# The order of three matmul terms in an MLP with split operands

## The chip, the core and the metric

The kernel runs on one core of a Trainium2 chip. The metric is the device time of the whole program in microseconds, from runs of the same program. One more execution was recorded by the hardware profiler, and everything that is said of instructions, waits and cadences is read from that record.

## What is computed

Sigmoid attention over 8 batches, 12 heads, 448 positions and a head size of 64, and then an MLP without biases on the 3584 rows that come out of it (768 to 2048 to 768, with a sigmoid-approximated GELU between):

```python
scores = scale * np.matmul(q, k.transpose(0, 1, 3, 2)) - np.log(S)
attn = 1.0 / (1.0 + np.exp(-scores))
x = np.matmul(attn, v)            # then (B, S, H * D) -> (3584, 768)
h = x @ w_in                      # 768 x 2048
g = h * (1.0 / (1.0 + np.exp(-1.702 * h)))
out = g @ w_out                   # 2048 x 768
```

## The kernel before, in words

The program has two halves. Up to about 253 us TensorE does the attention, while the other engines decode the weights. After that comes the MLP, which the change touches. The MLP does not multiply the matrices as they stand: it uses a fast bilinear scheme with 26 products per pair of blocks, so VectorE adds and subtracts blocks of the weights (`ws`, `kw`, `wf`), of the activations (`x`, `xs`, `kx` for the first matrix, `gs`, `kg`, `gl` for the second) and of the results (`h`, `o`). The table `SEQUENCE` lists 104 such products in the order in which TensorE takes them: two groups of tokens, two matrices, 26 products.

Each product needs two operands in more than one piece of precision. `split_piece` (lines 805 to 816) makes from a block of weights a tile `w` with a rounded part (index 0, "high", written by ScalarE at line 810 or VectorE at line 811) and what the rounding left (index 1, "low", a subtraction on VectorE at line 813, which can begin only when the high part is there). `pair_of` (lines 1021 to 1062) makes from a block of activations a tile `xp` (first matrix) or `gp` (second matrix) in the same way: high at lines 1040, 1041 or 1046, low on VectorE at line 1052 or 1054. Everything that is named `xp`, `gp` and `w` in the profile is such a tile.

`matmuls` (lines 841 to 848) then multiplies. For each 128x128 block of weights and each stretch of 448 columns of activations it issues three matmuls that add into the same place: the table `TERMS` (line 44) gives, for each of the three, which part of the weights (`a`) and which part of the activations (`d`) is read. Low times low is left out. A product is 36 matmuls in one go: 12 blocks by 3 terms. All 104 products together are 3744 matmuls with 128x128 weights, 1872 for each matrix.

The list scheduler `Plan.run` decides the order on each engine before anything runs, with its own estimates. A product's tasks on TensorE depend on the tasks that write the low parts, which come last, so the order is planned as if a product could begin only when both low parts are there. What each instruction waits for at run time is not set by the planner: it is put in afterwards, tile by tile and part by part, from what the instruction really reads. The matmul that reads a part first carries the wait for it, and everything behind it on TensorE's queue waits with it.

Other waits at the start of a product come from the accumulators: the two PSUM tiles `h0` and `h1` (named `p` in the profile) are used in turn, and a product can begin only when ScalarE or VectorE has read the one before it out (line 1228 a copy, 1262 an addition). Some products add to a value that ScalarE first copies in (lines 1186, 1188).

```python
            for j, (a, d) in enumerate(TERMS):
                nc.tensor.matmul(
                    ps, lhsT=ws(c // 6)[:, a, c % 6 * P : (c % 6 + 1) * P], rhs=x[:, d, k], start=start and i == 0 and j == 0,
                    stop=stop and i == len(todo) - 1 and j == 2, skip_group_check=True,
                )
```

Of the kernel before, what the change touches and what calls it, by code (L numbers as in the profile page):

```python
# [40 lines left out]
ISSUE, LANDING, PER_KB, MM = 0.43, (2.2, 2.5), 0.0027, 0.203  # L41
PIECE_RATE = dict(load=0.0032, save=0.0027)

TERMS = ((0, 1), (1, 0), (0, 0))

W_SUMS = ([(8, 0, 1, -1), (9, 5, 7, 1), (10, 3, 7, 1), (11, 0, 4, -1), (12, 0, 2, -1), (13, 6, 9, -1), (14, 4, 8, -1), (15, 6, 10, -1), (16, 2, 8, -1), (17, 10, 11, -1), (18, 4, 13, 1), (19, 3, 16, -1), (20, 9, 12, -1), (21, 6, 11, -1), (22, 6, 7, -1), (23, 5, 14, -1), (24, 1, 9, -1), (25, 2, 15, 1)], [(9, 1), (19, 1), (14, -1), (16, -1), (3, 1), (17, -1), (8, 1), (2, 1), (22, -1), (6, -1), (11, -1), (3, 1), (25, 1), (4, 1), (1, -1), (12, -1), (24, -1), (13, -1), (5, -1), (20, 1), (21, -1), (2, -1), (10, -1), (23, 1), (15, 1), (18, -1)])
X_SUMS = ([(8, 3, 7, 1), (9, 2, 6, 1), (10, 0, 3, 1), (11, 4, 6, -1), (12, 5, 9, 1), (13, 0, 8, 1), (14, 5, 6, 1), (15, 1, 3, -1), (16, 1, 8, -1), (17, 4, 9, -1), (18, 4, 13, 1), (19, 1, 12, 1), (20, 0, 17, 1), (21, 2, 10, -1), (22, 10, 14, 1), (23, 7, 11, 1), (24, 5, 16, 1), (25, 11, 15, 1)], [(9, -1), (14, 1), (13, 1), (22, 1), (5, -1), (16, 1), (10, -1), (21, 1), (11, 1), (20, 1), (8, 1), (23, 1), (15, 1), (0, 1), (18, 1), (19, 1), (5, 1), (17, 1), (4, -1), (12, -1), (1, -1), (1, -1), (24, -1), (7, -1), (25, 1), (2, 1)])
# [341 lines left out]
def sigmoid_attention_mlp(ctx: ExitStack, tc: tile.TileContext, qk, v, w, out):  # L389
# [451 lines left out]
    def matmuls(ps, ws, x, todo, start, stop):  # L841

        for i, (c, k) in enumerate(todo):
            for j, (a, d) in enumerate(TERMS):
                nc.tensor.matmul(  # L845
# [467 lines left out]
```

## Time and profile before

| | |
|---|---|
| median of the runs | 1045.49 us (2 runs, 1045.29 to 1045.7) |
| the profiled execution's own time | 1043.49 us |
| its span | 1041.7 us |
| granted clock of TensorE | 1.0 |
| matmuls and weight loads | 5588 and 5588 |
| busy share of PE, PEld, DVE, ACT | 98%, 80%, 90%, 56% |

PE is TensorE's matmuls and PEld its weight loads, which are recorded apart and overlap the matmuls. DVE is VectorE, ACT is ScalarE, SP issues the DMAs. A matmul's recorded duration is longer than the distance to the next one, because they are pipelined: the distance from start to start (here called the cadence) says what one costs. Idle time counts only where the chain of work that ends last runs through it.

### The profile page before, as it was taken

What the parts mean: (1) busy time and instruction counts of PE and PEld (TensorE: products, weight loads), DVE (VectorE), ACT (ScalarE), POOL (GpSimd) and SP (SyncE); (2) the same over time, 40 slices, a digit from 0 to 9 for tenths busy, and PEclk for the clock granted to TensorE, in tenths of its full rate; (3) what the DMA queues carried; (4) which work ended last, traced back from release to release, by engine and by line L of the source; (5) the groups of instructions that cost most, each with busy time, mean ns of one, the idle gap of its engine ahead of it and who ended that gap; (6) DMA issues with size and microseconds to landing.
All of it is one profiled execution on the core that took longest, in us unless ns stands there. A gap on an engine that the chain in (4) does not pass through costs nothing. (4 is left out here: it accounts for less than half of the span.)

```text
span 1041.7 us, 13721 instructions
## 1 busy us (share of the span) xinstructions
PE 1024.7 (98%) x5588; PEld 832.3 (80%) x5588; DVE 933.7 (90%) x654; ACT 588.4 (56%) x473; POOL 0.2 (0%) x4
## 2 busy tenths in 40 slices
PE   9999999999999999999999999999999999999998
PEld 5545454555898988888898898989999999999987
DVE  6998898897889988898899698999999999999896
ACT  6888887784454556545535445645563336454553
POOL 0000000000000000000000000000000000000000
PEclk9999999999999999999999999999999999999999
DMA  9999998879879878897997885966668389756755
GB/s 349 365 340 379 352 349 306 313 269 320 329 286 379 355 264 307 327 371 290 353 335 265 308 315 184 367 256 224 272 218 343 131 314 378 289 192 235 264 211 222
DMA packets 62799, 310.63 MB, mean 298 GB/s; under 512 B 6544, under 2 KB 14864, under 8 KB 58896
## 3 DMA queue, kind: packets, MB, share of 16 engines
q1 hardware_dynamic: 62736, 309.75, 79.4%
q8 instruction: 44, 0.72, 0.3%
q14 instruction: 19, 0.16, 0.0%
HBM read 200.38 MB, written 109.35 MB: 297 GB/s over the span
## 5 line engine op out<-in xcount | busy, mean ns | idle before, releaser
L845 PE MATMUL p<-xp,w 128*128 128x448 f32 x1872 | 386.1, 367 | 11.4 <-DVE xp L1052 7.5
L845 PEld LDWEIGHTS p<-xp,w 128*128 128x128 f32 x1872 | 349.8, 188 | 47.9 <-issue 10.2
L845 PE MATMUL p<-gp,w 128*128 128x448 f32 x1872 | 387.5, 368 | 0.3 <-DVE gp L1052 0.2
L845 PEld LDWEIGHTS p<-gp,w 128*128 128x128 f32 x1872 | 351.0, 188 | 36.3 <-issue 0.8
L635 ACT ACTIVATE a<-sc,bias 128x896 f32<-128x896 f32 x168 | 156.2, 1015 | 42.8 <-PE sc L665 26.2
L680 PE MATMUL av<-a,vraw 128*64 128x448 f32 x576 | 113.5, 543 | 0.0
L1228 ACT COPY h<-p 128x1792 f32<-128x1792 f32 x30 | 49.7, 1657 | 106.7 <-PE p L845 65.0
L1228 ACT COPY o<-p 128x1344 f32<-128x1344 f32 x37 | 47.1, 1283 | 101.8 <-PE p L845 95.5
L1262 DVE TENSOR_TENSOR h<-h,p 128x1792 f32<-128x1792 f32 x40 | 79.8, 2016 | 21.3 <-ACT h L1228 18.7
L649 PEld LDWEIGHTS sc<-qk 64*128 64x128 f32 x846 | 75.6, 184 | 27.7 <-PE sc L665 16.2
L649 PE MATMUL sc<-qk 64*128 64x448 f32 x846 | 94.7, 373 | 0.7 <-DVE x L710 0.7
L680 PEld LDWEIGHTS av<-a,vraw 128*64 128x64 f32 x576 | 39.2, 137 | 63.3 <-issue 46.8
L1262 DVE TENSOR_TENSOR o<-o,p 128x1344 f32<-128x1344 f32 x34 | 52.2, 1549 | 7.5 <-ACT o L1228 5.1
L1089 ACT ACTIVATE h<-h 128x1792 f32<-128x1792 f32 x28 | 47.5, 1702 | 14.5 <-DVE h L1262 14.5
L519 DVE TENSOR_TENSOR qk<-qkraw,qk 128x896 fp32r<-128x896 f32 x47 | 50.5, 1085 | 0.6
L1052 DVE TENSOR_TENSOR xp<-x,xp 128x1344 fp32r<-128x1344 f32 x26 | 40.4, 1552 | 8.1 <-ACT xp L1040 7.9
L710 DVE COPY x<-av 128x896 f32<-128x896 f32 x23 | 25.1, 1089 | 18.6 <-PE av L693 18.6
L1052 DVE TENSOR_TENSOR gp<-gs,gp 128x1792 fp32r<-128x1792 f32 x19 | 38.4, 2022 | 2.6 <-ACT gp L1040 2.2
L1052 DVE TENSOR_TENSOR gp<-kg,gp 128x1792 fp32r<-128x1792 f32 x18 | 36.3, 2019 | 1.7 <-ACT gp L1040 1.5
L813 DVE TENSOR_TENSOR w<-ws,w 128x1536 fp32r<-128x1536 f32 x19 | 33.3, 1752 | 1.3 <-ACT w L810 1.1
L514 DVE CAST qk<-qkraw 128x896 fp32r<-128x896 f32 x37 | 22.8, 622 | 12.4 <-DMA qkraw<-qk 6.1
L813 DVE TENSOR_TENSOR w<-kw,w 128x1536 fp32r<-128x1536 f32 x18 | 31.5, 1752 | 2.6 <-ACT w L810 2.6
(109 smaller groups left out, 931.8 us busy)
## 6 DMA issues: line engine op xcount, KB each, us to landing
w<-c SPq DMA_DIRECT2D x34, 768.0 KB, 5.8
w<-w SPq DMA_DIRECT2D x16, 1536.0 KB, 10.4
kg<-kg SPq DMA_DIRECT2D x27, 896.0 KB, 7.4
gl<-g SPq DMA_DIRECT2D x26, 896.0 KB, 7.4
x<-xd SPq DMA_DIRECT2D x34, 672.0 KB, 7.4
c<-w SPq DMA_DIRECT2D x14, 1536.0 KB, 8.0
qkraw<-qk SPq DMA_DIRECT2D x47, 448.0 KB, 6.3
kw<-kw SPq DMA_DIRECT2D x25, 768.0 KB, 7.4
```

What stands on the lines that cost most here:

```text
L514: (costs[1], lambda: nc.vector.tensor_copy(hi(), src())),
L519: lambda: nc.vector.tensor_tensor(lo(), src(), hi().bitcast(F32), op=ALU.subtract),
L635: nc.scalar.activation(a.tile, ps.tile[:, :, :S], AF.Sigmoid, bias=bias, scale=scale)
L649: nc.tensor.matmul(ps.tile[:, j, :S], lhsT=src[kk][rows, S + c * P : S + (c + 1) * P], rhs=src[qq][rows, :S], start=i == 0, stop=i == len( ...
L680: nc.tensor.matmul(ps.tile[cols, n % 2, :S], lhsT=vr.tile[:, at : at + D], rhs=a.tile[:, j], start=c == 0, stop=False, skip_group_check=True,)
L710: (1.09, lambda: nc.vector.tensor_copy(xb.tile, ps.tile[:, :, :S])), [t], [xb, ps], rows)
L813: t_lo = task("DVE", dve(n), lambda: nc.vector.tensor_tensor(into()[:, :, 1], src(), into()[:, :, 0].bitcast(F32), op=ALU.subtract), [t_hi ...
L845: nc.tensor.matmul(ps, lhsT=ws(c // 6)[:, a, c % 6 * P : (c % 6 + 1) * P], rhs=x[:, d, k], start=start and i == 0 and j == 0, stop=stop an ...
L1052: nc.vector.tensor_tensor(part(1)(), node.view(), part(0)().bitcast(F32), op=ALU.subtract)
L1089: t = task("ACT", act(GB), lambda: nc.scalar.activation(view(), node.view(), AF.Gelu_apprx_sigmoid, scale=float(sign)), [*node.done, *(nod ...
L1228: t = on_either((act(self.n), lambda: nc.scalar.copy(view(), node.view())), (dve(self.n), lambda: nc.vector.tensor_copy(view(), node.view())),
L1262: nc.vector.tensor_tensor(view(), x.view(), y.view(), op=ALU.add if s0 == s else ALU.subtract)
```

## The change

One line: the same three terms, in another order.

```diff
-TERMS = ((0, 1), (1, 0), (0, 0))
+TERMS = ((1, 0), (0, 0), (0, 1))
```

Before, each block goes high weights by low activations, low weights by high activations, high by high. Now it goes low weights by high activations, high by high, high weights by low activations. Two of the three matmuls, the second and the third, have the same weights one after the other; before, no two neighbours had. The first two share the activations, where before the last two did. Every matmul still brings its own weights: the program as built holds 5588 weight loads and 5588 matmuls on TensorE, as before. VectorE, ScalarE, GpSimd and SP have the same instructions in the same order.

What moves on TensorE's queue are the waits. The first place is the start of two products of the second matrix, of which the second is the one that begins at 688.07 us in the profile. (`p_1_16` is the accumulator of the product for token group 1, number 16; `gp_41` its activations, `w_2493` its weights; a name in brackets is the engine waited for.) Before:

```order
L845 MATMUL p_1_9_5574<-gp_12_5529,w_2647 128x448 [waits DVE_49,PE_49]
L845 MATMUL p_1_9_5574<-gp_12_5529,w_2647 128x448 [waits Activation_49]
L845 MATMUL p_1_9_5574<-gp_12_5529,w_2647 128x448 x34
L845 MATMUL p_1_16_5624<-gp_41_5591,w_2493 128x448 [waits DVE_49,PE_49]
L845 MATMUL p_1_16_5624<-gp_41_5591,w_2493 128x448 [waits Activation_49]
L845 MATMUL p_1_16_5624<-gp_41_5591,w_2493 128x448 x34
```

and now:

```order
L845 MATMUL p_1_9_5574<-gp_12_5529,w_2647 128x448 [waits DVE_49,Activation_49]
L845 MATMUL p_1_9_5574<-gp_12_5529,w_2647 128x448
L845 MATMUL p_1_9_5574<-gp_12_5529,w_2647 128x448 [waits DVE_49]
L845 MATMUL p_1_9_5574<-gp_12_5529,w_2647 128x448 x33
L845 MATMUL p_1_16_5624<-gp_41_5591,w_2493 128x448 [waits DVE_49,PE_49,Activation_49]
L845 MATMUL p_1_16_5624<-gp_41_5591,w_2493 128x448
L845 MATMUL p_1_16_5624<-gp_41_5591,w_2493 128x448 [waits DVE_49]
L845 MATMUL p_1_16_5624<-gp_41_5591,w_2493 128x448 x33
```

The wait for VectorE's low part of `gp` stood at the first matmul of a product and stands at the third now; the wait for ScalarE's high part moved from the second to the first.

The second place is near the end of the program, where the weights come last. Before:

```order
L845 MATMUL p_1_0_7739<-gp_42_7715,w_2647 128x448 [waits DVE_49,PE_49,Activation_49]
L845 MATMUL p_1_0_7739<-gp_42_7715,w_2647 128x448 x35
L845 MATMUL p_0_1_7787<-gp_18_7763,w_2493 128x448 [waits DVE_49,PE_49,Activation_49]
L845 MATMUL p_0_1_7787<-gp_18_7763,w_2493 128x448 [waits DVE_49]
L845 MATMUL p_0_1_7787<-gp_18_7763,w_2493 128x448 x34
```

and now:

```order
L845 MATMUL p_1_0_7739<-gp_42_7715,w_2647 128x448 [waits PE_49,Activation_49]
L845 MATMUL p_1_0_7739<-gp_42_7715,w_2647 128x448
L845 MATMUL p_1_0_7739<-gp_42_7715,w_2647 128x448 [waits DVE_49]
L845 MATMUL p_1_0_7739<-gp_42_7715,w_2647 128x448 x33
L845 MATMUL p_0_1_7787<-gp_18_7763,w_2493 128x448 [waits DVE_49,PE_49,Activation_49]
L845 MATMUL p_0_1_7787<-gp_18_7763,w_2493 128x448 x35
```

In the product `p_0_1` VectorE's last write is the low part of the weights. The wait for it stood at the second matmul and stands at the first now, and since VectorE works in order it covers the low part of the activations too.

## The prediction

> **What bounds the kernel now.** I read the page first: its shares, and the groups of the two kinds of product.
>
> ```profile
> span 1041.7 us, 13721 instructions
> PE 1024.7 (98%) x5588; PEld 832.3 (80%) x5588; DVE 933.7 (90%) x654; ACT 588.4 (56%) x473; POOL 0.2 (0%) x4
> ...
> L845 PE MATMUL p<-xp,w 128*128 128x448 f32 x1872 | 386.1, 367 | 11.4 <-DVE xp L1052 7.5
> L845 PEld LDWEIGHTS p<-xp,w 128*128 128x128 f32 x1872 | 349.8, 188 | 47.9 <-issue 10.2
> L845 PE MATMUL p<-gp,w 128*128 128x448 f32 x1872 | 387.5, 368 | 0.3 <-DVE gp L1052 0.2
> L845 PEld LDWEIGHTS p<-gp,w 128*128 128x128 f32 x1872 | 351.0, 188 | 36.3 <-issue 0.8
> ```
>
> One load is recorded for each matmul, 188 ns long, and the change touches 3744 of them, 386.1 + 387.5 = 774 us of TensorE's time. VectorE at 90% is the next engine. Then the chain that ended last:
>
> ```profile
> 650.98 37.04 PE p L845 x180
> 688.02 0.06 issue
> 688.07 297.85 PE p L845 x1440
> 985.92 0.02 issue
> 985.94 1.29 ACT o L1228
> 987.25 1.56 DVE o L1262
> ...
> 1014.22 1.68 DVE w L813
> 1015.90 0.04 issue
> 1015.94 22.39 PE p L845 x107
> ```
>
> TensorE alone sets the pace from 650.98 to 985.92 and after 1015.94. Between these, VectorE does, and its low part of the weights (line 813) lets TensorE go for the last time. How full both are, by stage:
>
> ```profile
> core 0: us, PE busy (x) PEld busy (x) DVE busy (x) ACT busy (x) POOL busy (x), PEclk, DMA share, GB/s
> 253.50:651.00 397.50, 386.09 (x1877) 349.87 (x1873) 351.36 (x219) 193.76 (x130) 0.00 (x0) 1.00 0.83 312
> 688.00:986.00 298.00, 297.93 (x1443) 270.61 (x1443) 283.23 (x162) 143.79 (x104) 0.00 (x0) 1.00 0.68 257
> 986.00:1016.00 30.00, 29.73 (x146) 26.79 (x144) 28.75 (x18) 17.05 (x13) 0.00 (x0) 1.00 0.65 238
> ```
>
> VectorE has 46 us of air in the first stage (397.5 − 351.4), 14.8 us in the second and hardly any after. Last, TensorE's cadence, by stretches without a wait:
>
> ```profile
> 606.00:648.00 42.00, 42.00 (x209) 1.00 0.73 257
> 652.00:680.00 28.00, 28.00 (x140) 1.00 0.91 357
> 689.00:837.00 148.00, 148.00 (x718) 1.00 0.62 236
> 837.00:985.00 148.00, 148.00 (x718) 1.00 0.73 276
> ```
>
> A window counts also the matmuls that reach over its edges, 367/204 = 1.8 of them. So the cadence is 42.00/207.2 = 202.7 ns and 28.00/138.2 = 202.6 ns in the first two rows, and 148.00/716.2 = 206.6 ns in both halves of the long stretch. The instructions have the same shapes and the clock is 1.00 throughout: there are two cadences, 4.0 ns apart, and the slow one held for 296 us without a break.
>
> **The load of equal weights.** The change makes two neighbours share their weights in 3744/3 = 1248 places. It pays only if the second load is dropped or becomes cheaper. The trace has one place where neighbours have the same weights, the 26 matmuls at the program's start that read one tile `still`:
>
> ```profile
> L442 PEld LDWEIGHTS <-still 128*128 128x128 bf16 x26 | 2.7, 148 | 1.0 <-DVE bias L445 1.0
> ```
>
> All 26 loads are there. The changed program too carries one load for each matmul. So I cost this part at nothing. Its bounds: a load begins at the matmul before and takes 188 ns of the 206.6 to the next one, so what a dropped load could free is, as an estimate from these rows, the 18.6 ns of handing over, 1248 × 18.6 = 23.2 us. The other bound is nothing saved. Nothing here gives a price above zero for a load whose length and port stay as they are.
>
> The Trainium skill ("TensorE: Matmul & The Clock Gate", section "Back-to-back issue gap") gives a lone warm matmul N/2.4 + 2.5 ns, which is 189.2 ns for 448 columns, and for streams of load and matmul about 131 ns at 512 columns. The trace agrees with neither, at 202.7 and 206.6 ns. By the first figure a dropped load would save, as an estimate, 17.4 ns, 21.7 us in all. The same page ("What happens when you issue a matmul") says that the next weights load into a background buffer while the matmul before still runs; by that rule a load costs a long matmul nothing, and sparing it gains nothing.
>
> **The waits that move.** These are the certain effect. At the start of a product the low part of the activations is needed at the third matmul instead of the first, so it may come two matmuls, 2 × 0.205 = 0.41 us (0.205 lies between the two cadences), later without a stall. Who waited for it:
>
> ```profile
> PE p L845 <- DVE xp L1052: 7.5, 10, 1.7
> ...
> PE p L845 <- DVE gp L1052: 0.2, 1, 0.2
> PE p L845 <- DVE xp L1054: 0.2, 1, 0.2
> ```
>
> That is 12 starts, 7.9 us in all. A matmul is recorded 0.16 us longer than the cadence (367 − 205 ns), so each lost 0.16 us more than its row says. Nearly all lost over 0.41 us, so at most 12 × 0.41 = 4.9 us are saved. Against that, the low part of the weights is needed at the first matmul instead of the second, one matmul earlier:
>
> ```profile
> PEld p L845 <- DVE w L813: 2.4, 3, 1.4
> ```
>
> Three starts each lose a matmul that ran under the wait, 3 × 0.205 = 0.6 us. One of them also takes back a saving:
>
> ```profile
> 382.17 0.44 PE L845 MATMUL p<-xp,w 128*128 128x448 f32 x1 [0.17 <-DVE xp L1052]
> 383.75 29.53 PE L845 MATMUL p<-xp,w 128*128 128x448 f32 x143 [1.14 <-DVE w L813]
> ```
>
> Here the first matmul waited 0.17 us for `xp` and the second 1.14 for `w`; now both wait for `w`, and the 0.17 + 0.16 = 0.3 us saved at the first are lost.
>
> How much of 4.9 − 0.3 = 4.6 us reaches the end? If VectorE's times were fixed, TensorE would only stand longer at the next wait: nothing. If VectorE follows TensorE, all. In the first stage VectorE waits too, and for TensorE at one remove:
>
> ```profile
> ACT h L1228 <- PE p L845: 65.0, 17, 11.2
> DVE h L1262 <- ACT h L1228: 22.1, 11, 6.7
> ```
>
> ScalarE's copies of results wait for TensorE, and VectorE's additions wait 22.1 us for these copies, half of its 46 us of air. So VectorE is let go earlier where TensorE is. I take 0.6 of 4.6 us, −2.8 us, and of the 0.6 us lost +0.4, since the one at 1015.94 lies on the chain's end and counts in full. Sum −2.4 us, between +0.6 and −4.6. Queued behind such a wait is only the rest of the product; VectorE, ScalarE and SP keep their order.
>
> **The cadence.** I don't know what sets it. Between waits it does not change: both halves of the long stretch agree to the count. The chain shows 0.06 us of "issue" at 688.02 ahead of that stretch, a wait far shorter than 0.41 us, which goes away, because the low part that it waited for is wanted two matmuls later. Then TensorE would run on from 652 us at the cadence that it had there, 202.6 ns. Over 1433 matmuls (716.2 twice) that is 1433 × 4.0 = 5.7 us less. VectorE must follow: it has 14.8 us of air in the stage, but 28.75 of 30.0 us are full after 986, so I keep 4.0 us of it. Other end: the cadence stays slow, nothing.
>
> **The sum.** The profiled execution took 1043.5 us (span 1041.7 and 1.8 around it); the median of the runs is 1045.5, so 2.0 us go on top. With both terms: −2.4 − 4.0 = −6.4 us, 1037.1, on the runs' scale 1039.
>
> **The rivals.**
>
> *Waits alone.* The long stretch keeps 206.6 ns, because some other short wait falls before it, or because the cadence belongs to the stretch and not to the wait. For it: the slow cadence fills the long stretch, which holds most products of the second matrix and few of the first. Then −2.4 us: 1043. Chance 0.32.
>
> *The second load is dropped or runs free.* For it: the loads are 188 ns of a 203 to 207 ns cadence, so they may be what sets it. Against it: 26 loads of one tile at the start, none left out. 1045.5 − 23.2 = 1022 at the lowest, and VectorE's air of 14.8 us in the long stretch leaves room for the 480 × 18.6 = 8.9 us that it would lose there. Chance 0.03. The skill's figure, above, is near this price and its other rule is against it.
>
> *Slower: the fast stretches turn slow.* The mechanism is the same as in my forecast with the other sign. TensorE starts again after a wait at the slow cadence where it was at the fast one, in the first stage, which has 1877 matmuls, and in the 37 us after. The price is 4.0 ns each, at most (3744 − 1433) × 4.0 = 9.2 us. It decides from 2.4/0.0040 = 600 more slow matmuls on, where the gain of the waits is used up. At worst 1045.5 − 2.4 + 9.2 = 1052. For it: waits get moved at nearly every product, so every start is dealt anew. Against it: both cadences stand in the trace, and the long stretch is slow already. Chance 0.12.
>
> *VectorE's times are fixed.* All that TensorE saves it waits for later, and the wait for `w` at 1015.94 adds 0.2 us: 1045.7. For it: VectorE is full after 986. Against it: its own waits on ScalarE's copies. Chance 0.05.
>
> **How the numbers follow.** My forecast, both terms, has 0.48, and the time is its 1039. Its bounds are −4.6 − 5.7 (1035) and +0.6 with no cadence (1046). The range from 1034 to 1048 takes in the waits-alone case, fixed VectorE times and the nearer half of the slow rival; the dropped load and the far half are left out, about 1 in 10. A measurement of this kernel tells about 2% (21 us) from no change. Only the dropped load reaches it: faster 0.03. No case that I can price reaches 1066, so slower gets 0.02 for what I haven't seen, and within 2% gets 0.95.
>
> **What would show it.** Right: 5588 loads again, 188 ns long; the waits of PE for `xp` at line 1052 fall from 7.5 us to about 4; a wait for `w` at line 813 now ahead of a product's first matmul, 0.2 us later at the end; and no wait near 688, with 1435 matmuls in about 290 us. Wrong: fewer loads than matmuls, or a cadence under 200 ns every third matmul (the load was dropped); the same waits for `xp` (VectorE fixed); 206.6 ns before 680 (the slow rival). A time outside 1034 to 1048 with both cadences unchanged would mean that I have missed a wait.

## The result, and the profile after

The changed kernel took 1034.8 us (1034.57 to 1035.04, 2 runs) against 1045.49 us: a ratio of 0.9898, interval 0.9855 to 0.994. That is 10.7 us less, more than the 6.5 us that I forecast. Most of the surplus was chance, as the repeats below show: over more runs of both the ratio is 0.9951 (0.9933 to 0.9969), 5.1 us.

The page of the changed kernel, the lines that answer to those of before:

```profile
span 1033.3 us, 13713 instructions
PE 1018.3 (99%) x5588; PEld 832.3 (81%) x5588; DVE 933.0 (90%) x654; ACT 588.3 (57%) x473; POOL 0.2 (0%) x4
...
L845 PE MATMUL p<-xp,w 128*128 128x448 f32 x1872 | 387.1, 367 | 8.8 <-DVE xp L1052 3.5
L845 PEld LDWEIGHTS p<-xp,w 128*128 128x128 f32 x1872 | 349.8, 188 | 46.1 <-DVE xp L1052 7.3
L845 PE MATMUL p<-gp,w 128*128 128x448 f32 x1872 | 380.9, 365 | 0.8 <-DVE w L813 0.8
L845 PEld LDWEIGHTS p<-gp,w 128*128 128x128 f32 x1872 | 351.2, 188 | 29.9 <-issue 1.4
```

There are as many loads as before, and they are as long. The matmuls of the second matrix (`gp`) are 6.6 us shorter in sum (387.5 to 380.9). The chain that ended last:

```profile
648.63 0.06 issue
648.69 328.94 PE p L845 x1620
977.64 0.02 issue
977.66 1.29 ACT o L1228
...
1005.94 1.68 DVE w L813
1007.62 0.14 issue
1007.75 22.14 PE p L845 x108
```

Read against the chain of before, this says where the 8.4 us between the two spans went. The product that began at 650.98 begins at 648.69: 2.3 us earlier. TensorE's stretch up to the copy by ScalarE, 334.94 us before (650.98 to 985.92), is 328.95 us long: another 6.0 us. VectorE's stage behind it is as long as it was (985.92 to 1015.94, now 977.64 to 1007.75, 30.0 and 30.1 us). The last wait now stands ahead of 108 matmuls instead of 107. The 6.0 us are the cadence, in the windows of the changed kernel (time, busy time, number of matmuls):

```profile
652.00:680.00 28.00, 28.00 (x139) 1.00 0.92 353
690.00:837.00 147.00, 147.00 (x728) 1.00 0.63 242
837.00:975.00 138.00, 138.00 (x681) 1.00 0.73 276
```

With the 1.8 matmuls at the edges taken off, that is 147.00/726.2 = 202.4 and 138.00/679.2 = 203.2 ns where there were 206.6 ns (the second window holds two short waits, near 839 and 861 us). The waits of TensorE for VectorE:

```profile
PE p L845 <- DVE xp L1052: 3.5, 5, 0.7
PE p L845 <- DVE w L813: 3.5, 3, 1.7
```

Those for `xp` fell from 7.5 us in 10 to 3.5 us in 5, and those for `w` rose from 1.1 us in one to 3.5 us in 3. Part of that rise is where they are counted: before, two more waits for `w` showed in the row of the loads alone (2.4 us in 3).

### The profile page after: what moved, and what is told of

It is laid out like the page before. It is cut to its first block, busy times and chain, and to the rows that moved or that the text cites. A ratio compares the mean times of both kernels' runs of the same rounds, so it can differ in the third digit from the quotient of the medians.

```text
span 1033.3 us, 13713 instructions
## 1 busy us (share of the span) xinstructions
PE 1018.3 (99%) x5588; PEld 832.3 (81%) x5588; DVE 933.0 (90%) x654; ACT 588.3 (57%) x473; POOL 0.2 (0%) x4
## 4 chain that ended last, share of the span: by engine, by line
PE 46%; DVE 4%; ACT 1%; issue 1%; DVEq 0%; ACTq 0%
PE p L845 46%; DVE gp L1052 1%; DVE o L1262 1%; DVE w L813 1%; DVE kg L788 1%; DVE h L1262 0%; ACT p L1186 0%; DVE x L788 0%; DVE h L1229 0%; DVE wf L788 0%; ACT h L1228 0%; ACT o L1228 0%; DVE gp L1041 0%; ACT o L1116 0%; DVEq L813 0%
## 5 line engine op out<-in xcount | busy, mean ns | idle before, releaser
L845 PE MATMUL p<-gp,w 128*128 128x448 f32 x1872 | 380.9, 365 | 0.8 <-DVE w L813 0.8
L1262 DVE TENSOR_TENSOR h<-h,p 128x1792 f32<-128x1792 f32 x40 | 79.8, 2017 | 20.7 <-ACT h L1228 18.2
L649 PEld LDWEIGHTS sc<-qk 64*128 64x128 f32 x846 | 75.6, 184 | 27.6 <-PE sc L665 16.2
L710 DVE COPY x<-av 128x896 f32<-128x896 f32 x23 | 25.1, 1091 | 17.2 <-PE av L693 17.1
```

The costliest lines, as they stand in the source:

```text
L649: nc.tensor.matmul(ps.tile[:, j, :S], lhsT=src[kk][rows, S + c * P : S + (c + 1) * P], rhs=src[qq][rows, :S], start=i == 0, stop=i == len( ...
L710: (1.09, lambda: nc.vector.tensor_copy(xb.tile, ps.tile[:, :, :S])), [t], [xb, ps], rows)
L845: nc.tensor.matmul(ps, lhsT=ws(c // 6)[:, a, c % 6 * P : (c % 6 + 1) * P], rhs=x[:, d, k], start=start and i == 0 and j == 0, stop=stop an ...
L1262: nc.vector.tensor_tensor(view(), x.view(), y.view(), op=ALU.add if s0 == s else ALU.subtract)
```

## The experiments

Theory A is that of the prediction: a load costs the same whichever weights it brings, and the time moves because the waits moved, with the cadence of the stretches behind them. Theory B is that the second load of equal weights is cheaper. All ratios are to the kernel before, on the same chip; its own median was 1041.53 us (35 runs) beside e0_before_again, e0_after_again, e1_waits and e2_share, 1040.84 us (16 runs) beside e0_after_third, e3, e4_terms_outer and e5, and 1043.46 us (12 runs) beside e4_again and e6.

| kernel | median us | range | ratio (95%) |
|---|---|---|---|
| e0_before_again | 1041.57 | 1037.83 to 1044.93 | 1.0008 (0.9989 to 1.0026) |
| e0_after_again | 1036.05 | 1033.28 to 1041.19 | 0.9951 (0.9933 to 0.9969) |
| e0_after_third | 1035.59 | 1033.81 to 1037.88 | 0.995 (0.9931 to 0.997) |
| e1_waits | 1036.37 | 1033.91 to 1042.36 | 0.9965 (0.9946 to 0.9984) |
| e2_share | 1040.86 | 1037.91 to 1044.78 | 0.9996 (0.9978 to 1.0013) |
| e3_high_first | 1038.04 | 1032.19 to 1039.93 | 0.9963 (0.9941 to 0.9984) |
| e4_terms_outer | 1029.93 | 1028.76 to 1038.39 | 0.9906 (0.9876 to 0.9936) |
| e4_again | 1031.82 | 1029.14 to 1036.79 | 0.990 (0.9876 to 0.9923) |
| e5_half_outer | 1033.97 | 1029.57 to 1037.38 | 0.992 (0.9892 to 0.9948) |
| e6_one_block | 1035.34 | 1033.43 to 1040.17 | 0.9932 (0.9905 to 0.9958) |

**The two parts of the change, each alone.** In e1_waits and e2_share the first of a product's 12 blocks goes in one order and the other 11 in the other. The first block decides all the waits, which in e1_waits are those of the changed kernel and in e2_share those of the kernel before, instruction by instruction; the other 11 decide how many neighbours share their weights. (Not shown: `lead`, which tells `matmuls` that it is at the start of a product.)

```diff
-TERMS = ((0, 1), (1, 0), (0, 0))
+LEAD_TERMS, TERMS = ((1, 0), (0, 0), (0, 1)), ((0, 1), (1, 0), (0, 0))  # e1_waits; e2_share the other way round
...
-            for j, (a, d) in enumerate(TERMS):
+            for j, (a, d) in enumerate(LEAD_TERMS if lead and i == 0 else TERMS):
...
```

> The first of a product's 12 blocks goes in the new order, the other 11 in the old one: all waits stand where the change puts them, but only 104 of the 1248 pairs of neighbours with equal weights are left. Theory A (the waits moved, and with them where TensorE starts again and at which cadence): about the time of the changed kernel, 1035 us, within 4 us, with 202.7 ns in the long stretch from about 686 to 980 us if the cadence follows the start, and 206.6 ns there and about 1041 us if that was luck. Theory B (the second load of equal weights is cheaper): a twelfth of the gain is left, about 1044.6 us.

> The first block of each product in the old order, the other 11 in the new one: all waits stand where the kernel before has them, and 1144 of the 1248 pairs with equal weights are there. Theory A: the time of the kernel before, 1043.5 to 1045.5 us, unless the cadence of the long stretch comes out fast, then about 1039. Theory B: eleven twelfths of the gain of 10.7 us, so about 1035.7 us, and a cadence in the long stretch below 206.6 ns by 5.

Theory A holds for both. With 104 of the 1248 pairs left but the waits moved, e1_waits gains 0.35%; with 1144 pairs but the old waits, e2_share gains nothing that 12 runs can see (0.9978 to 1.0013). Theory B asked for the opposite. The times that I had expected for e2_share, 1043.5 to 1045.5 us, were missed (1040.86), because the kernel before is itself faster over more runs (1041.53). The two have the waits that they should have. From the pages, e1_waits and then e2_share:

```profile
L845 PE MATMUL p<-xp,w 128*128 128x448 f32 x1872 | 388.4, 368 | 9.7 <-DVE xp L1052 4.0
```

```profile
L845 PE MATMUL p<-xp,w 128*128 128x448 f32 x1872 | 385.7, 367 | 11.3 <-DVE xp L1052 7.4
```

4.0 us for `xp` beside 3.5 in the changed kernel, and 7.4 beside 7.5 in the kernel before.

**The same programs once more.** No edit: the kernel before and the changed one, for a second and third profile.

> The kernel before, once more. If the cadence of a stretch belongs to the program (where TensorE starts again after which wait), the long stretch has 206.6 ns again and the same stretches as before are slow. If it is drawn anew in each execution, some of the stretches change, each slow one with about 0.3 to 0.5, and the time moves by up to 6 us between executions.

> The changed kernel, once more, with 5 rounds for the interval. Cadence of the program: 202.7 ns in the long stretch again and about 1034.8 us. Drawn anew: with about a third the long stretch is slow, and that execution takes about 1040.5 us.

> The changed kernel once more, for the interval and for a third look at the cadence. Dealt anew in each execution: 0.995 of the kernel before, within 0.002, and the long stretch slow in about a third to a half of the executions, which makes two groups of times some 5.7 us apart.

The cadence of a stretch is not fixed by the program: it is dealt anew in each execution. In the changed kernel's second profile the long stretch is slow (windows of e0_after_again):

```profile
652.00:680.00 28.00, 28.00 (x139) 1.00 0.93 353
690.00:837.00 147.00, 147.00 (x713) 1.00 0.62 237
837.00:984.00 147.00, 147.00 (x713) 1.00 0.73 276
```

147.00/711.2 = 206.7 ns, where the first profile of the same program had 202.4 and 203.2. This execution took 1040.82 us, the first 1035.04. In the other direction, e2_share, which has the waits of the kernel before, ran the first part of the stretch fast and the second slow within one execution (windows of e2_share):

```profile
690.00:800.00 110.00, 110.00 (x544) 1.00 0.70 270
845.00:985.00 140.00, 140.00 (x679) 1.00 0.72 272
```

These are 110.00/542.2 = 202.9 and 140.00/677.2 = 206.7 ns. The other two came out in the long stretch as the first profiles of their programs: e0_before_again slow (147.00/711.2 = 206.7 ns twice), e0_after_third fast, behind a short stretch that is slow there and fast in the other four profiles of the two programs (windows of e0_after_third):

```profile
652.00:680.00 28.00, 28.00 (x137) 1.00 0.93 358
690.00:837.00 147.00, 147.00 (x726) 1.00 0.63 240
```

These are 28.00/135.2 = 207.1 and 147.00/724.2 = 203.0 ns. The third set of runs of the changed kernel kept the ratio that was expected (0.995), but not the two groups of times: all six lie between 1033.81 and 1037.88 us.

Counted over the start times of all twelve profiles, 255 stretches of at least 25 matmuls lie between two waits (places where a matmul starts more than 214 ns after the one before): 185 ran at the fast cadence, 67 at the slow one, and 3 changed on the way. Which places are slow differs between executions of one program.

Where does it change? In the kernel before, the slow cadence did not begin at 688 us but one product earlier. Up to 680.1 us the matmuls start 202.7 ns apart, from 680.6 us on 206.7. The loads of the kernel before wait at both places:

```profile
680.30 7.32 PEld L845 LDWEIGHTS p<-gp,w 128*128 128x128 f32 x36 [0.25 <-issue]
688.04 12.07 PEld L845 LDWEIGHTS p<-gp,w 128*128 128x128 f32 x59 [0.42 <-PE p L845]
```

Between two loads at the slow cadence 0.02 us are idle (207 − 188 ns), so these came 0.23 and 0.40 us late. In the changed kernel the first of the two waits is gone, and near 686 us one is left in two of its three profiles. The loads there, in the profile that came out fast and then in the one that came out slow:

```profile
685.69 3.34 PEld L845 LDWEIGHTS p<-gp,w 128*128 128x128 f32 x17 [0.23 <-DVE gp L1052]
```

```profile
685.49 3.60 PEld L845 LDWEIGHTS p<-gp,w 128*128 128x128 f32 x18 [0.23 <-DVE gp L1052]
```

In both, the load of the third matmul waits for the low part of `gp`. The matmul itself is only 10 to 24 ns late (it starts 227 and 217 ns after the one before, where 203 to 207 is usual), but the one behind it is late by another 0.1 us (310 and 308 ns), so that 0.12 to 0.13 us are lost in all. The stretch behind it is dealt again: fast in one profile, slow in the other.

In e0_after_third no matmul is late there. But the load of that third matmul starts 71 ns after the matmul before it, where 2 to 3 ns is usual, and at this place, 687.2 us, the cadence goes from 206.7 to 202.7 ns. So the loads tell more than the matmuls. In all twelve profiles a load normally starts 1 to 6 ns after the matmul before. Divided at every load that starts more than 20 ns after it (the first three matmuls behind such a load not counted), the matmuls of the MLP fall into 269 stretches of at least 25, and each of them keeps one cadence to its end: 197 fast, 72 slow. No change of cadence was seen but at a late load, though at many late loads it did not change.

**Other orders.** If only the waits count, an order with no equal neighbours at all must gain as much, and one that wants the low parts later must gain more. In e3_high_first the terms are high by high, low weights, low activations. In e4_terms_outer the loops over blocks and terms are exchanged as well, so that each term goes through all blocks of an output tile. In e5_half_outer they are exchanged over half a product (its loops stand elsewhere in the kernel and are not shown).

```diff
-TERMS = ((0, 1), (1, 0), (0, 0))
+TERMS = ((0, 0), (1, 0), (0, 1))                # e3_high_first, e4_terms_outer, e5_half_outer
...
-        for i, (c, k) in enumerate(todo):
-            for j, (a, d) in enumerate(TERMS):
+        for j, (a, d) in enumerate(TERMS):      # e4_terms_outer
+            for i, (c, k) in enumerate(todo):
...
```

> Terms in the order high by high, low weights by high activations, high weights by low activations: no neighbours have equal weights, the low part of the activations is wanted at the third matmul as in the changed kernel, the low part of the weights at the second as in the kernel before. Theory A (only the waits count): the gain of the changed kernel plus up to 0.6 us, so about 5 us under the kernel before (0.995). Theory B (equal weights pay): no gain from weights, at most 3 us (0.997 to 1.0). The cadence of each stretch is dealt anew in each execution.

> As e3_high_first, but within the 9 matmuls of one output tile (6 for the second matrix, twice) all blocks go through a term before the next term begins: the low part of the weights is wanted at the 4th (3rd) matmul, the low part of the activations at the 7th (5th). Neighbours never have equal weights. Theory A: waits of up to 1.2 us (0.8 us) for the activations are covered, and most of the about 10 waits of 0.7 us for xp that the changed kernel still has go away: 4 to 7 us less than the changed kernel where TensorE sets the pace, of which VectorE, full at the end, may keep half: ratio to the kernel before about 0.990 to 0.994. Theory B: as e3_high_first.

> As e4_terms_outer, over half a product: 6 matmuls high by high, 6 with the low weights, 6 with the low activations. The low weights are wanted at the 7th matmul (1.2 us later), the low activations at the 13th (2.5 us later, more than the 1.5 to 2.0 us that VectorE takes to make them). Theory A: nearly all of TensorE's waits for xp, gp and w go away; what is left are the accumulators and VectorE at the end. 3 to 6 us less than e4_terms_outer if VectorE follows, the same as e4_terms_outer if VectorE is the bound by then. Theory B: as e3_high_first.

> e4_terms_outer once more, for its interval and its two groups: ratio 0.989 to 0.993, single times about 1029 to 1031 where the stretch from 646 us to the end runs at 202.7 ns, and about 1036 to 1038 where it runs at 206.6 ns (1870 matmuls by 4.0 ns is 7.5 us).

e3_high_first gains 0.37% without one pair of equal weights; its interval (0.9941 to 0.9984) takes in the changed kernel's ratio and e1_waits's. Alone it would not decide between the theories, since B allowed 0.997. Its waits (TensorE for VectorE):

```profile
PE p L845 <- DVE xp L1052: 3.1, 5, 0.9
PE p L845 <- DVE w L813: 2.8, 3, 1.5
```

e4_terms_outer is faster than both kernels, 0.9906 and 0.990 in two goes. Its waits for `xp` are nearly gone (e4_again; 1.0 us in 2 in the other profile):

```profile
PE p L845 <- ACT p L1186: 3.2, 3, 1.5
PE p L845 <- DVE w L813: 3.0, 3, 1.7
...
PE p L845 <- DVE xp L1052: 0.5, 1, 0.5
```

What is left is the waits for `w` and for the values that ScalarE copies in (line 1186). The second kind no order of the terms covers, because the first matmul already adds to these values. Its 12 runs lie in two groups, 1028.8 to 1032.8 us (9 runs) and 1036.6 to 1038.4 us (3 runs). The two profiles show why, over the same 332 us, first e4_again (1029.14 us), then e4_terms_outer (1038.39 us):

```profile
648.00:814.00 166.00, 166.00 (x821) 1.00 0.70 269
814.00:980.00 166.00, 166.00 (x821) 1.00 0.73 276
```

```profile
648.00:814.00 166.00, 166.00 (x805) 1.00 0.69 263
814.00:980.00 166.00, 166.00 (x805) 1.00 0.72 270
```

16 matmuls more in each window, 166.00/819.2 = 202.6 ns against 166.00/803.2 = 206.7. In the slow one the chain that ended last stays on TensorE from 646 us on, with VectorE ahead of it all the way.

e5_half_outer covers still more and is no faster than e4_terms_outer (0.992, interval 0.9892 to 0.9948, with three of its six runs at 1035.7 to 1037.4). The second outcome expected for it holds, though for another reason than VectorE: the waits that it covers in addition are few (5.9 us of TensorE's waits in the MLP are left, where the two profiles of e4 have 6.6 and 7.6), and its profile is one with a slow stretch to the end. How much faster it is at the same cadence isn't settled by six runs.

**Nearly all weights equal.** In e6_one_block the waits are those of the changed kernel, but from the second block on every matmul reads the same 128x128 block of high weights in each half of the tile. It leaves out the multiplication by all the other blocks.

```diff
+                a, cc = (a, c) if lead and i == 0 else (0, c // 6 * 6)
...
-                    ps, lhsT=ws(c // 6)[:, a, c % 6 * P : (c % 6 + 1) * P], rhs=x[:, d, k], ...
+                    ps, lhsT=ws(cc // 6)[:, a, cc % 6 * P : (cc % 6 + 1) * P], rhs=x[:, d, k], ...
```

> The changed kernel with its waits, but from the second block of a product on every matmul reads one and the same 128x128 block of the high weights per half of the tile: 33 of 36 matmuls have the weights of the matmul before (or change them once), where the changed kernel has 12 of 36. This leaves out the multiplication by the other blocks of the weights, so the numbers computed are not the MLP's. Theory A (a load costs the same whichever weights it brings): cadences of 202.7 and 206.6 ns and no others, 3744 loads of 188 ns, and the time of the changed kernel, 1033 to 1041 us. Theory B (equal weights are cheaper): cadence towards 190 ns, and a time some 20 to 40 us lower where VectorE allows it.

Groups of the page and two windows of e6_one_block:

```profile
L846 PEld LDWEIGHTS p<-xp,w 128*128 128x128 f32 x1872 | 350.0, 188 | 45.1 <-DVE xp L1053 7.0
...
L846 PEld LDWEIGHTS p<-gp,w 128*128 128x128 f32 x1872 | 351.0, 188 | 32.5 <-issue 1.4
```

```profile
690.00:800.00 110.00, 110.00 (x544) 1.00 0.68 264
...
864.00:984.00 120.00, 120.00 (x582) 1.00 0.70 266
```

All 3744 loads are there, 188 ns each, and the cadences are 202.9 ns (110.00/542.2) and 206.8 ns (120.00/580.2): the two that the kernel has anyway. Its time is that of the changed kernel within the intervals (0.9932, 0.9905 to 0.9958). This settles theory B: with 33 of 36 loads bringing what is there already, nothing is saved. The figure that the prediction took from the Trainium skill ("TensorE: Matmul & The Clock Gate", section "Back-to-back issue gap"), 189.2 ns, was not reached here either. What the prediction took from the same page's "What happens when you issue a matmul", that the next weights load while the matmul before still runs, agrees with these rows: a load of 188 ns for each matmul fits into a cadence of 203 to 207 ns.

## Why the prediction was right or wrong

**The load of equal weights, costed at nothing: right.** e2_share and e6_one_block show it, and the 26 loads of `still` were the right row to read it from.

**The waits, −2.4 us: right in size.** The cadence can be taken out by counting only what is lost at waits: for every matmul of the MLP that starts more than 214 ns after the one before, the time beyond 204.5 ns. That is 17.4, 18.2 and 18.2 us in the three profiles with the old waits (the kernel before twice, e2_share) and 14.9, 16.2 and 16.0 us in the three of the changed kernel: 2.2 us less. The spread is wide: e1_waits, with the same waits, lost 17.2 us. The saving for `xp` and the loss for `w` came about as priced: 7.5 to 3.5 us where I had said about 4, and `w` ahead of a product's first matmul. I left out one cost: behind a stalled matmul the next one starts 276 to 315 ns later in most cases, so that each stall loses 0.07 to 0.11 us more.

**The cadence, −4.0 us: came in this profile, but the step to it was wrong.** I had it that a short wait near 688 us sets the slow cadence, that it goes away, and that TensorE then runs on at the cadence that it had. Three things in that were wrong. The slow cadence began at the wait before, at 680.3 us, which my window, ended at 680.00, did not show. The wait at 688 was not 0.06 us long, as I read from the chain, but 0.40 us at the load, as long as the 0.41 us that two matmuls cover, and 0.12 to 0.13 us of loss were left there in two of three profiles. And a late load deals the cadence anew, without setting a certain one: the long stretch came out fast in the first profile and slow in the second. So the term is not an effect that the change is shown to have: it is a draw, 5.7 us wide, made in each execution of either kernel. I could have seen the risk: the row of the long stretch was one observation of one execution, and I read it as belonging to the program.

**What VectorE lets through: too low.** I kept 4.0 of 5.7 us, because VectorE is full after 986 us. VectorE's stage kept its length, 30.0 and 30.1 us, and began earlier by all that TensorE had gained.

**The sum.** 6.5 us were forecast, 10.7 measured first and 5.1 over more runs. The first comparison set two runs near the top of what the kernel before does (1037.2 to 1046.0 us over 63 later runs) against two in the lower half of the changed kernel's (1033.3 to 1041.2 us over 18 later runs). That 1039 lies between is no merit: the sum had one term of the right size and one that was a draw. Nor do the waits alone make up the 5.1 us (interval 3.2 to 7.0 us). In the six profiles named above the times differ by 5.9 us in the mean: 2.2 us are the waits, 1.0 us is there already when the MLP begins (at 252.9 us instead of 254.0 in the mean), and 2.6 us is the cadence: about 1820 of the 3744 matmuls ran slow with the old waits and 1160 in the changed kernel, 660 times 4.0 ns. Within each three the slow matmuls range from 1320 to 2080 and from 680 to 1830. So whether the changed kernel also deals slow stretches less often isn't settled, and why its attention half, which the change does not touch, ended earlier stays open.

**The rivals.** Waits alone, −2.4 us, has the mechanism that the experiments show, though 2.4 us lie below the interval of the gain. The dropped load is refuted. Fixed times on VectorE are refuted by the stage that kept its length. The rival on the slow side is real as a draw: the changed kernel's longest runs reach 1041 us, but the kernel before has the same draws.

## What to carry to other kernels

Order the terms of a split product by when their operands get ready, not by which operand stays: the part that is computed last goes last, and as far back as the waits for it are long (here 1% with the terms outside the blocks, half of that with the order of three alone, and nothing more that six runs could see with them still further out). A wait of a few tenths of a microsecond at the head of a group is covered by each matmul that can go ahead without the late operand. And before a stretch's pace in one profile is put down to the program, look at a second profile of the same program: here a difference of 2% in cadence belonged to the execution.

## What the runs showed of the hardware that was not expected

Matmuls of one shape (128x128 weights, 448 columns) with the granted clock at 1.00 run at one of two cadences, 202.7 or 206.7 ns. In 252 of 255 stretches between waits the cadence held to the end, for up to 387 us; 185 were fast and 67 slow. It changed only where a weight load came late: divided at the loads that start more than 20 ns after the matmul before (1 to 6 ns is normal), none of 269 stretches changes. A load that started 71 ns after the matmul before, with no matmul delayed, was enough (e0_after_third), and a late load does not always change it. Both cadences were seen with equal weights (e6_one_block), in every order of the terms, and with the same share of busy DMA engines (0.63 fast and 0.62 slow in the window from 690 us of the changed kernel). What decides between the two stays open: no run here steered it. For this kernel it is worth more than the change: single runs of one program spread over 8 us, and of e4_terms_outer over 9.6 us.
